# Gate and value weights split without scaling in place, and the low halves of block zero's M made on TensorE

## The chip, the core and the metric

One core of a Trainium2 chip. The metric is device microseconds of one execution, and the time of a kernel is the median of its runs. Engines are named as in the profile: PE is TensorE (PEld its weight loads), DVE is VectorE, ACT is ScalarE, POOL is GpSimd, SP is the queue that issues most DMAs.

## What is computed

Three stages, each over the output of the one before.

```python
scores = scale * x @ state^T;  a  = softmax(scores);   xread = a @ state     # B=8, H=8, S=512, D=64
scores2 = scale * state @ x^T; a2 = softmax(scores2);  sread = a2 @ x        # Ns=32
x = concat([xread, sread], axis=2) -> 4352 rows of 512
x = (sigmoid(x @ w_gate) * (x @ w_val)) @ w_out                              # 512 -> 1536 -> 512
e = argmax(x @ w_gate2);  y = softmax(x @ w_gate2)[e] * relu(x @ w1[e]) @ w2[e]   # 8 experts, 512 -> 1024 -> 512
```

The three weights of the middle stage arrive as 64-bit floats, read here as pairs of 32-bit words.

## The kernel before

Every product keeps near fp32 accuracy by splitting both operands into a high and a low float16 half and summing three products (high x high, high x low, low x high) in PSUM. To split, an operand is scaled by a power of two from its largest magnitude. `pair` (L310) does it: ScalarE writes the high half, and the low half is the difference. With `s` and not `inplace` the difference is one VectorE operation that scales and subtracts (L319). With `inplace` ScalarE first scales the fp32 operand where it lies (L313), casts it (L315), and POOL subtracts (L316).

**Weights.** Gate and value weights come in six pairs of 256 columns (`fp` = 0 to 5). `load_wgv` (L519) loads a pair raw, into regions of `wgv` and `wout` that are not yet in use. `conv_wgv` (L532) is a generator of two steps. The first joins the words with three VectorE operations per half (L499, L502, L505, each 128x1024) into a buffer of the tag `big` or `out`, and squares it on ScalarE for the largest magnitude (L540). The second spreads the maximum through a TensorE matmul (`spread`, L199), makes the scale on VectorE (L154 to L158) and calls `pair` in place (L546). The output weights go the same way in twelve pieces of 128x512 (`conv_wout`, L551), with one scale over all of them, so the scaled halves (L589, L590) come only after all twelve are joined.

**Tokens.** The rows of `xread` are not formed. For each batch b the state is multiplied into the weights instead: `state_weights` (L468) makes M, for a pair fp, by 24 small matmuls of 64x32 weights (L483) into two PSUM banks; ScalarE evacuates each bank as the high half (L490), VectorE as the low half (L491). `gate_val` (L659), for one of twelve column groups fc, multiplies M with the transposed attention aT in twelve matmuls of 512 columns (L665 to L667), six for gate and six for value. ScalarE applies the sigmoid (L671), VectorE multiplies (L673), ScalarE casts the high half (L678) and POOL subtracts the low half (L679). Four output products of 36 matmuls each follow (`mlp_out`, L717). PSUM for these is one pool of four banks (`mm_p`, L171); a gate product takes two, an M two.

**Order.** TensorE's order is the program's. `token_block` (L1095) writes it: calls of `gate_val` with a hook `mid` in the middle and at the end of each, in which numbered slots start steps of the next block's attention and of background work. On the other engines a planner orders the instructions from modelled times; each queue runs in that order.

**Block zero** (b = 0) is special: its M is made inside the loop over fc, just before its use, at each even fc (L1166 to L1172), and the weights of pair fp + 2 are converted in the same loop: the first step at fc = 2 fp (L1174, L1175), the second at fc = 2 fp + 1 (L1179). Pairs 0 and 1 are converted ahead of it (L1193 to L1201). From slot 13 on the hooks also run `conv_wout`; what is left of it is issued before the output products (L1182). For b > 0 the six Ms of the next block are made in slots GV + 2m, among the output products (L1131).

**Row metadata.** In the expert stage each tile of 128 rows has a small tile `meta` (eight of them, L874) that a DMA on SP fills (L883), and that a VectorE operation (L921) and the indirect DMA that stores the rows (L924) read.

Of the kernel before, what the change touches and what calls it, by code (L numbers as in the profile page):

```python
# [10 lines left out]
F16 = mybir.dt.float16  # L11
# [8 lines left out]
P = 128  # L20
# [6 lines left out]
def attention_moe_router_kernel(  # L27
# [49 lines left out]

    ACT_SH = 23

    SC_SH = 22  # L80

    PR_SH = 14

# [19 lines left out]
    identf = const.tile([P, P], F32, name="identf", tag="identf")  # L103
    ident = const.tile([P, P], F16, name="ident", tag="ident")
    identb = const.tile([P, P], BF16, name="identb", tag="identb")
    tri = const.tile([P, P], F16, name="tri", tag="tri")
    ones = const.tile([P, 1], F16, name="ones", tag="ones")
    iota_e = const.tile([P, NE], F32, name="iota_e", tag="iota_e")
# [22 lines left out]
        kw = {} if bufs is None else {"bufs": bufs}  # L131
        return (pool or tiny).tile(shape, dt, name=name, tag=name, **kw)

    def pow2_scale(m, k, nm, lim=40, inv=True, bufs=None, out=None):

        n = m.shape[1]
        a = tl([P, n], I32, nm + "a")
        s = tl([P, n], I32, nm + "s", bufs) if out is None else out.bitcast(I32)
        nc.vector.tensor_scalar(a, m.bitcast(I32), EXPO, EXPO, ALU.bitwise_and, ALU.bitwise_xor)
        nc.vector.tensor_scalar(  # L140
            s, a, float((128 + lim) * ONE), float((k - 1) * ONE), ALU.min, ALU.add
        )
        if not inv:
            return s.bitcast(F32), None
        c = tl([P, n], I32, nm + "c", bufs)
        nc.vector.tensor_scalar(c, s, -1.0, float(254 * ONE), ALU.mult, ALU.add)
        return s.bitcast(F32), c.bitcast(F32)

    def pow2_scale_sq(q, c, nm):
# [86 lines left out]
    def state_max(b):  # L236

        g = states[b]
        m = tl([P, 1], name="sgm")
        nc.vector.tensor_reduce(  # L240
            m, g["st"].rearrange("p r d -> p (r d)"), axis=AX.X, op=ALU.max,
            apply_absolute_value=True,
        )
        yield
        r = all_max(spread(m), "sgr")
        g["s"], g["i"] = pow2_scale(r, 14, "sg", bufs=3)

        bf = att.tile([64, H // 2, 2, D], F32, name="bf", tag="a")
        bd = att.tile([64, 2, H // 2, 2, D], F16, name="bd", tag="sT")
        bsh = [64, H // 2, 2, D]  # L250
        nc.gpsimd.tensor_tensor(
            bf, g["st"][0:64].unsqueeze(2).to_broadcast(bsh),
            hmask[0:64].unsqueeze(3).to_broadcast(bsh), op=ALU.mult,
        )
        bw = bd.rearrange("p l r i d -> p l (r i d)")
        pair(bf.rearrange("p r i d -> p (r i d)"), bw[:, 0], bw[:, 1], g["s"][0:64])
        g["bd"] = bd
        yield
# [28 lines left out]
    def unit_max(n):  # L287
# [13 lines left out]

        for nm in ("c1", "c2", "c3", "n1"):
            u[nm] = tl([P, 1], name="s" + nm, bufs=3)
        nc.vector.tensor_scalar(u["c1"], i, g["i"], SCALE, ALU.mult, ALU.mult)
        nc.vector.tensor_scalar(u["n1"], u["c1"], -1.0, None, ALU.mult)
        nc.vector.tensor_scalar(u["c2"], u["c1"], 2.0 ** SC_SH, None, ALU.mult)
        nc.vector.tensor_scalar(u["c3"], i, 2.0 ** -PR_SH, None, ALU.mult)
# [160 lines left out]
    def state_weights(b, fp):  # L468

        Mt[b, fp] = m_p.tile([P, NU, 2, 2, FP], F16, name="M", tag="M")
        pm = [mm_ps([P, 2, FP]) for c in range(NU)]
        bdT = states[b]["bdT"]
        for m, l in ((0, 0), (0, 1), (1, 0)):
            for r in range(NP):
                for h in range(2):
                    for c in range(NU):  # L480
                        k = slice(64 * h, 64 * h + 64)
                        o = NS * (h ^ c)
                        nc.tensor.matmul(  # L483
                            pm[c][64 * r + o:64 * r + o + NS],
                            bdT[k, m, NP * c + r, o:o + NS], wgv[k, fp, l, :, NP * c + r, :],
                            start=(m + l == 0), stop=(m == 1),
                        )
        t = Mt[b, fp]
        for c in range(NU):
            last["A"] = nc.scalar.activation(t[:, c, 0], pm[c], AF.Copy, scale=2.0 ** -M_SH)  # L490
            last["D"] = nc.vector.scalar_tensor_tensor(  # L491
                t[:, c, 1], pm[c], 2.0 ** -M_SH, t[:, c, 0], op0=ALU.mult, op1=ALU.subtract
            )


    def convert64(dst, raw):
# [35 lines left out]
    def conv_wgv(fp, raws):  # L532
# [10 lines left out]
        both = inv_w.rearrange("p k (a i) -> p k a i", i=2)[:, :, fp]  # L543
        s = pow2_scale_sq(r, both, "ws")
        for k in range(2):
            pair(v[k], h[k][0], h[k][1], s[:, k:k + 1], inplace=True)  # L546
        yield

    wo_sq = const.tile([P, NFC], F32, name="wo_sq", tag="wo_sq")
# [314 lines left out]
            nc.sync.dma_start(out=dst, in_=src, **kw)  # L864

    rows = {}
    xgT = {}

    def place_rows(s, late=False):
        if late:  # L870
            xgT[s] = m_p.tile([P, 2, NDC, P], F16, name="M", tag="M")
        else:
            xgT[s] = big([P, 2, NDC, P], F16)
        rows[s] = const.tile([P, 16], I32, name=f"meta{s % 8}", tag=f"meta{s % 8}")  # L874

    def fetch_rows(s, r0):
        if s not in xgT:
# [61 lines left out]
    make_identity(nc, identf)  # L939
    nc.vector.tensor_copy(ident, identf)  # L940
    nc.vector.tensor_copy(identb, identf)
    hm_i = tl([P, H // 2, 2], I32, "hm_i")

    nc.gpsimd.iota(
# [150 lines left out]
    def token_block(b):  # L1095
# [8 lines left out]
        if b + 1 < B:  # L1104
# [23 lines left out]
                at(EARLY, lambda: first_step(NU * (b + 2)))  # L1128
                at(EARLY + 2, lambda: unit_load(NU * (b + 2) + 1))
            for m in range(NFP):  # L1130
                at(GV + 2 * m, lambda m=m: state_weights(b + 1, m))  # L1131
        if b + 1 == B:
            rs = state_rows()
            at(6, lambda: next(rs, None))
# [30 lines left out]
        for fc in range(NFC):  # L1165
            if b == 0 and fc % 2 == 0:  # L1166
                fp = fc // 2
                state_weights(0, fp)
                nc.vector.tensor_scalar(
                    sg[:, fc:fc + 2], inv_w[:, 0, fc:fc + 2], isig, 2.0 ** (M_SH - PR_SH),  # L1170
                    ALU.mult, ALU.mult,
# [6 lines left out]
            elif b == 0 and fc // 2 + 2 < NFP:  # L1178
                drain(deque([cvs.pop(fc // 2 + 2)]))  # L1179
            gate_val(fc, S, sg, V_SH, token_chunks(b, fc), acts, mid)  # L1180
        if b == 0:
            drain(bg)  # L1182
        rt_new(b, isig)
# [284 lines left out]
```

## Time and profile before

| what | value |
|---|---|
| median of 3 runs | 1202.6 us (1199.43 to 1203.38) |
| the profiled execution | 1203.0 us |
| its span, first to last instruction | 1201.3 us |
| mean granted clock of TensorE | 0.952 of full |
| TensorE matmul busy in the span | 1077.0 us, 90% |
| VectorE busy | 858.8 us, 71% |
| ScalarE busy | 560.1 us, 47% |
| POOL busy | 310.1 us, 26% |

The profile comes from one execution. Rows give start and duration in microseconds from the span's start, with the line of the kernel; names are of tiles, `out<-in`. In square brackets stands how long the engine had been idle before an instruction and what ended that. A group's row gives its count, its busy time, the mean of one in ns and the idle time before its members. Matmuls overlap in their pipeline, so the listed duration of one is longer than its step to the next. The granted clock is a share of 2.4 GHz.

### The profile page before, as it was taken

To read this page: it belongs to the slowest core of one execution; us is meant where nothing else is said; L and a number is where in the kernel's file an instruction comes from. 1 tells how busy PE (TensorE), PEld (TensorE's weight loads), DVE (VectorE), ACT (ScalarE), POOL (GpSimd) and SP (SyncE) were. 2 spreads that over 40 slices of the span, in tenths; PEclk is the share of its full clock that TensorE was granted. 3 is DMA by queue.
4 is the path that set the end of the run, shared out by engine and by line. 5 is a ranking of instruction groups with operands and counts; after the bars stand their busy time and mean duration, and the time that the engine had idled before them with its cause. 6 is when DMAs were issued, how large, how long until landed. Compare 5 with 4: busy or idle time off the path is not lost. (4 is left out here: it accounts for less than half of the span.)

```text
span 1201.3 us, 22322 instructions
## 1 busy us (share of the span) xinstructions
PE 1077.0 (90%) x8303; PEld 589.6 (49%) x8303; DVE 858.8 (71%) x2079; ACT 560.1 (47%) x967; POOL 310.1 (26%) x305
## 2 busy tenths in 40 slices
PE   2265659889899999999999999999999999999997
PEld 1221224434344444344444444867666667776674
DVE  6878996688787887887877765447656666565564
ACT  3566563774776857767678483311111111111111
POOL 1244310350532524415235071301100000000000
PEclk9576779999999999999999999999999999999999
DMA  7422566545756667557465652473312495979348
GB/s 254 162 71 88 158 114 120 124 162 140 218 168 176 224 142 216 167 159 237 121 207 158 159 195 95 139 232 120 88 42 50 109 357 127 312 248 366 81 82 292
DMA packets 187745, 200.65 MB, mean 167 GB/s; under 512 B 130159, under 2 KB 154735, under 8 KB 184304
## 3 DMA queue, kind: packets, MB, share of 16 engines
q1 hardware_dynamic: 172736, 147.51, 45.0%
q0 software_dynamic: 14896, 51.67, 11.3%
q8 instruction: 67, 1.10, 0.4%
q14 instruction: 46, 0.38, 0.1%
HBM read 217.40 MB, written 54.88 MB: 227 GB/s over the span
## 5 line engine op out<-in xcount | busy, mean ns | idle before, releaser
L910 ACT CAST acth<-v 128x256 f16<-128x256 f32 x148 | 59.9, 404 | 331.2 <-DVE v L909 308.3
L679 POOL TENSOR_TENSOR actl<-g,acth 128x512 f16<-128x512 f32 (+1 forms) x108 | 138.7, 1286 | 161.8 <-ACT acth L678 161.3
L665 PE MATMUL mm<-aT,M 128*128 128x512 f16 x384 | 152.8, 398 | 26.1 <-ACT M L490 19.9
L722 PE MATMUL mm<-wout,acth 128*128 128x512 f16 x408 | 156.2, 383 | 9.1 <-DVE wout L590 8.8
L667 PE MATMUL mm<-aT,M 128*128 128x512 f16 x384 | 152.2, 396 | 11.5 <-DVE M L491 11.5
L723 PE MATMUL mm<-wout,acth 128*128 128x512 f16 x408 | 156.0, 382 | 0.0
L724 PE MATMUL mm<-wout,actl 128*128 128x512 f16 x408 | 155.8, 382 | 0.0
L666 PE MATMUL mm<-aT,M 128*128 128x512 f16 x384 | 152.7, 398 | 0.0
L895 PEld LDWEIGHTS <-wgv 128*128 128x128 f16 x1184 | 115.6, 98 | 20.0 <-DMA wgv<-w_d 2.8
L924 POOL DMA_INDIRECT out_dram<-g,meta x37 | 35.9, 972 | 344.5 <-DVE g L921 286.7
L895 PE MATMUL mm<-big,wgv 128*128 128x256 f16 x704 | 118.5, 273 | 1.5 <-DMA wgv<-w_d 1.5
L898 PEld LDWEIGHTS <-wgv 128*128 128x128 f16 x1184 | 115.8, 98 | 3.8
L898 PE MATMUL mm<-big,wgv 128*128 128x128 f16 x704 | 117.4, 219 | 0.0
L908 DVE TENSOR_REDUCE v<-mm 128x256 f32<-128x512 f32 x148 | 101.4, 685 | 19.8 <-PE mm L898 18.8
L911 DVE TENSOR_TENSOR actl<-v,acth 128x256 f16<-128x256 f32 x148 | 62.8, 424 | 68.6 <-ACT acth L910 68.6
L319 DVE SCALAR_TENSOR_TENSOR out<-big,inv,out 128x1024 f16<-128x1024 f32 x64 | 83.5, 1305 | 36.7 <-ACT out L318 36.7
L673 DVE SCALAR_TENSOR_TENSOR g<-mm,g 128x512 f32<-128x512 f32 (+1 forms) x108 | 70.9, 657 | 53.3 <-PE mm L667 27.3
L318 ACT ACTIVATE out<-big,inv 128x1024 f16<-128x1024 f32 x64 | 73.2, 1144 | 52.6 <-DVE inv L140 45.5
L671 ACT ACTIVATE g<-mm,sgf 128x512 f32<-128x512 f32 (+1 forms) x108 | 71.2, 660 | 43.5 <-POOL actl L679 26.4
L650 POOL DMA_DIRECT2D w_d<-out x63 | 35.5, 563 | 189.3 <-DVE out L319 138.1
L678 ACT CAST acth<-g 128x512 f16<-128x512 f32 (+1 forms) x108 | 63.3, 588 | 40.8 <-DVE g L673 40.6
L895 PE MATMUL mm<-out,wgv 128*128 128x256 f16 x480 | 80.8, 273 | 0.0
(320 smaller groups left out, 2152.3 us busy)
## 6 DMA issues: line engine op xcount, KB each, us to landing
wgv<-w_d SPq DMA_DIRECT2D x56, 2048.0 KB
wout<-w_d SPq DMA_DIRECT2D x18, 2048.0 KB
big<-in_moe_w_dram SPq DMA_DIRECT2D x64, 512.0 KB
w_d<-out POOLq DMA_DIRECT2D x64, 512.0 KB, 4.9
xb<-in_x_dram SPq DMA_DIRECT2D x60, 128.0 KB
wgv<-in_moe_w_gate_dram SPq DMA_DIRECT2D x3, 1024.0 KB
wgv<-in_moe_w_val_dram SPq DMA_DIRECT2D x3, 1024.0 KB
wout<-in_moe_w_gate_dram SPq DMA_DIRECT2D x3, 1024.0 KB
```

The lines of the kernel that those rows point to most:

```text
L318: nc.scalar.activation(h16, v, AF.Copy, scale=s)
L319: nc.vector.scalar_tensor_tensor(l16, v, s, h16, op0=ALU.mult, op1=ALU.subtract)
L665: nc.tensor.matmul(ps[k], w[0], v[0], start=(i == 0), stop=False)
L666: nc.tensor.matmul(ps[k], w[0], v[1], start=False, stop=False)
L667: nc.tensor.matmul(ps[k], w[1], v[0], start=False, stop=(i == len(parts) - 1))
L679: last["P"] = nc.gpsimd.tensor_tensor(lo, g, h, op=ALU.subtract)
L722: nc.tensor.matmul(po, hj, wout[:, fc, 1], start=(fc == 0), stop=False)
L723: nc.tensor.matmul(po, hj, wout[:, fc, 0], start=False, stop=False)
L724: nc.tensor.matmul(po, lj, wout[:, fc, 1], start=False, stop=(fc == NFC - 1))
L895: nc.tensor.matmul(ph[:, i], w1s[:, pr, c, 0, f], t[:, :, c], start=(c == 0), stop=False)
L898: nc.tensor.matmul(ph[:, i, 1], w1s[:, pr, c, 1, f], t[:, 0, c], start=False, stop=(c == NDC - 1),)
L908: nc.vector.tensor_reduce(v, ph.rearrange("p i l q -> p i q l"), axis=AX.X, op=ALU.add)
```

## The change

The change has four parts.

1. `conv_wgv` calls `pair` without `inplace`: ScalarE scales and writes the high half in one pass, and VectorE makes the low half (L319's operation) from the unscaled operand. L313, L315 and POOL's L316 are no longer issued for the gate and value weights.
2. `state_weights` becomes a generator of two steps. The first makes the product and lets ScalarE write the highs; for b > 0 VectorE writes the lows there as before, and callers run both steps at once. For b = 0 the second step takes two more banks, multiplies the highs by a negative scaled identity (`minus`) into them, adds the same product again and lets ScalarE write the lows.
3. In block zero M of pair 0 is made whole before the first `gate_val`; the first step for pair fp + 1 comes after `gate_val(2 fp)`, the second after `gate_val(2 fp + 1)`.
4. So that the negative identity fits float16, the state is scaled by 2^6 less (`ST_SH`), and constants are adapted. The eight `meta` tiles become slices of one tile of tag `xT`.

```diff
-    SC_SH = 22
+    ST_SH = 6
+
+    SC_SH = 22 - ST_SH
...
+    minus = const.tile([P, P], F16, name="minus", tag="minus")
...
-        g["s"], g["i"] = pow2_scale(r, 14, "sg", bufs=3)
+        g["s"], g["i"] = pow2_scale(r, 14 - ST_SH, "sg", bufs=3, sh=ST_SH)
...
+        bdT = states[b]["bdT"]
+        t = Mt[b, fp]
+        down = 2.0 ** (ST_SH - M_SH)
+
+        def product(pm, first):
+            for m, l in ((0, 0), (0, 1), (1, 0)):
+                for r in range(NP):
+                    for h in range(2):
+                        for c in range(NU):
+                            k = slice(64 * h, 64 * h + 64)
+                            o = NS * (h ^ c)
+                            nc.tensor.matmul(
+                                pm[c][64 * r + o:64 * r + o + NS],
+                                bdT[k, m, NP * c + r, o:o + NS], wgv[k, fp, l, :, NP * c + r, :],
+                                start=(first and m + l == 0), stop=(m == 1),
+                            )
+
         pm = [mm_ps([P, 2, FP]) for c in range(NU)]
...
+        product(pm, True)
         for c in range(NU):
-            last["A"] = nc.scalar.activation(t[:, c, 0], pm[c], AF.Copy, scale=2.0 ** -M_SH)
-            last["D"] = nc.vector.scalar_tensor_tensor(
-                t[:, c, 1], pm[c], 2.0 ** -M_SH, t[:, c, 0], op0=ALU.mult, op1=ALU.subtract
-            )
+            last["A"] = nc.scalar.activation(t[:, c, 0], pm[c], AF.Copy, scale=down)
+            if b > 0:
+                last["D"] = nc.vector.scalar_tensor_tensor(
+                    t[:, c, 1], pm[c], down, t[:, c, 0], op0=ALU.mult, op1=ALU.subtract
+                )
+        yield
+        if b == 0:
+            pm = [mm_ps([P, 2, FP]) for c in range(NU)]
+            for c in range(NU):
+                nc.tensor.matmul(pm[c], minus, t[:, c, 0], start=True, stop=False)
+            product(pm, False)
+            for c in range(NU):
+                nc.scalar.activation(t[:, c, 1], pm[c], AF.Copy, scale=down)
...
-            pair(v[k], h[k][0], h[k][1], s[:, k:k + 1], inplace=True)
+            pair(v[k], h[k][0], h[k][1], s[:, k:k + 1])
...
-        rows[s] = const.tile([P, 16], I32, name=f"meta{s % 8}", tag=f"meta{s % 8}")
+        if "all" not in meta:
+            meta["all"] = att.tile([P, 8, 16], I32, name="meta", tag="xT")
+        rows[s] = meta["all"][:, s % 8]
...
+    nc.vector.tensor_scalar(minus, identf, -(2.0 ** (M_SH - ST_SH)), None, ALU.mult)
...
-                at(GV + 2 * m, lambda m=m: state_weights(b + 1, m))
+                at(GV + 2 * m, lambda m=m: drain(deque([state_weights(b + 1, m)])))
...
-                state_weights(0, fp)
+                if fp == 0:
+                    ws = state_weights(0, 0)
+                    drain(deque([ws]))
...
             gate_val(fc, S, sg, V_SH, token_chunks(b, fc), acts, mid)
+            if b == 0 and fc + 2 < NFC:
+                if fc % 2 == 0:
+                    ws = state_weights(0, fc // 2 + 1)
+                next(ws, None)
```

## Rows read from the trace of the kernel before

**Rows 1.** The page, span in forty slices: busy share of each in tenths.

```profile
PE   2265659889899999999999999999999999999997
```

**Rows 2.** Windows: stretch, length, busy by engine, granted clock, DMA share, GB/s.

```profile
60.00:105.00 45.00, 26.73 (x153) 9.06 (x151) 35.96 (x52) 30.27 (x45) 20.82 (x11) 0.66 0.18 59
105.00:165.00 60.00, 31.59 (x201) 10.92 (x199) 51.78 (x112) 37.73 (x68) 19.62 (x12) 0.75 0.43 127
...
180.00:240.00 60.00, 56.65 (x498) 26.75 (x495) 39.71 (x143) 31.71 (x53) 13.20 (x11) 0.97 0.56 121
```

**Rows 3.** Waits of PE, 60 to 165: us in total, times, longest.

```profile
PE mm L665 <- ACT M L490: 19.9, 6, 6.8
PE mm L667 <- DVE M L491: 11.5, 7, 3.0
PE mm L483 <- ACT g L671: 3.7, 1, 3.7
```

**Rows 4.** Timeline of PE: start, us, instruction, idle before it and releaser.

```profile
57.45 2.72 PE L451 MATMUL at<-a2T,xn 128*128 128x64 f16 x48 [4.92 <-ACT a2T L442]
...
60.42 1.48 PE L483 MATMUL mm<-wgv,bdT 64*32 64x512 f16 x24
64.97 0.61 PE L665 MATMUL mm<-aT,M 128*128 128x512 f16 x1 [3.07 <-ACT M L490]
...
165.14 0.61 PE L722 MATMUL mm<-wout,acth 128*128 128x512 f16 x1 [6.96 <-DVE wout L590]
```

**Rows 5.** Timeline of ACT, the same columns.

```profile
55.35 1.06 ACT L540 ACTIVATE wgv<-big 128x1024 f16<-128x1024 f32 x1 [7.21 <-DVE big L505]
...
89.72 1.15 ACT L313 ACTIVATE big<-big,wss 128x1024 f32<-128x1024 f32 x1 [3.34 <-DVE wss L157]
```

**Rows 6.** Timeline of all engines, 45 to 55.

```profile
48.09 4.71 DVE L499 TENSOR_SCALAR big<-wgv 128x1024 int32<-128x1024 int32 x1 [0.72 <-POOL wgv L316]
...
50.12 2.12 POOL L316 TENSOR_TENSOR wgv<-big,wgv 128x1024 f16<-128x1024 f32 x1
```

**Rows 7.** Instructions of lines L499, L505, L319: shortest, median, longest in ns, first and last start.

```profile
L499 DVE TENSOR_SCALAR wout<-out x6: 407/414/1608, 103.8 to 129.5; 128x512 int32<-128x512 int32 x6
...
L499 DVE TENSOR_SCALAR big<-wout x2: 680/1344/2008, 89.7 to 96.9; 128x1024 int32<-128x1024 int32 x2
L499 DVE TENSOR_SCALAR out<-wout x1: 2598/2598/2598, 68.1 to 68.1; 128x1024 int32<-128x1024 int32 x1
...
L499 DVE TENSOR_SCALAR big<-wgv x1: 2214/2214/2214, 85.2 to 85.2; 128x1024 int32<-128x1024 int32 x1
...
L505 DVE SCALAR_TENSOR_TENSOR wout<-out,wout x6: 671/680/2058, 106.0 to 136.0; 128x512 int32<-128x512 int32 x6
...
L505 DVE SCALAR_TENSOR_TENSOR big<-wout,big x2: 1226/2129/3032, 93.4 to 101.1; 128x1024 int32<-128x1024 int32 x2
...
L319 DVE SCALAR_TENSOR_TENSOR bd<-bf,sgs,bd x2: 744/1610/2475, 8.3 to 132.5; 64x512 f16<-64x512 f32 x2
```

**Rows 8.** Groups of POOL by form, 60 to 165: busy, mean ns, idle before.

```profile
L679 POOL TENSOR_TENSOR actl<-g,acth 128x512 f16<-128x512 f32 x12 | 17.4, 1451 | 36.4 <-ACT acth L678 36.4
L316 POOL TENSOR_TENSOR wgv<-big,wgv 128x1024 f16<-128x1024 f32 x6 | 13.8, 2321 | 11.5 <-ACT wgv L315 11.5
L316 POOL TENSOR_TENSOR wgv<-out,wgv 128x1024 f16<-128x1024 f32 x4 | 9.3, 2344 | 17.0 <-ACT wgv L315 16.9
```

**Rows 9.** Groups of ACT by form, 60 to 165, the same columns.

```profile
L490 ACT ACTIVATE M<-mm 128x512 f16<-128x512 f32 x14 | 7.8, 587 | 0.0
```

**Rows 10.** Groups of DVE by form, 60 to 165, the same columns.

```profile
L491 DVE SCALAR_TENSOR_TENSOR M<-mm,M 128x512 f16<-128x512 f32 x14 | 9.3, 680 | 1.1 <-ACT M L490 1.1
L673 DVE SCALAR_TENSOR_TENSOR g<-mm,g 128x512 f32<-128x512 f32 x12 | 8.2, 684 | 7.1 <-PE at L199 3.4 <-PE mm L667 2.9 <-ACT g L671 0.8
L505 DVE SCALAR_TENSOR_TENSOR wout<-out,wout 128x512 int32<-128x512 int32 x6 | 6.8, 1129 | 0.0
```

**Rows 11.** Waits of the SP queue, 60 to 180.

```profile
SPq L557 <- POOL wgv L316: 33.3, 4, 23.9
```

More of the change, by code (lines that the diff above doesn't have):

```diff
@@ L132, in tl, with pow2_scale @@
         return (pool or tiny).tile(shape, dt, name=name, tag=name, **kw)
-    def pow2_scale(m, k, nm, lim=40, inv=True, bufs=None, out=None):
+    def pow2_scale(m, k, nm, lim=40, inv=True, bufs=None, out=None, sh=0):
         n = m.shape[1]
@@ L145, in pow2_scale @@
         c = tl([P, n], I32, nm + "c", bufs)
-        nc.vector.tensor_scalar(c, s, -1.0, float(254 * ONE), ALU.mult, ALU.add)
+        nc.vector.tensor_scalar(c, s, -1.0, float((254 - sh) * ONE), ALU.mult, ALU.add)
         return s.bitcast(F32), c.bitcast(F32)
@@ L303, in unit_max @@
             u[nm] = tl([P, 1], name="s" + nm, bufs=3)
-        nc.vector.tensor_scalar(u["c1"], i, g["i"], SCALE, ALU.mult, ALU.mult)
+        nc.vector.tensor_scalar(u["c1"], i, g["i"], SCALE * 2.0 ** ST_SH, ALU.mult, ALU.mult)
         nc.vector.tensor_scalar(u["n1"], u["c1"], -1.0, None, ALU.mult)
@@ L474, in state_weights @@
         Mt[b, fp] = m_p.tile([P, NU, 2, 2, FP], F16, name="M", tag="M")
-        pm = [mm_ps([P, 2, FP]) for c in range(NU)]
[L476 to L486, printed above, removed]
-                        )
@@ L488, in state_weights @@
-        t = Mt[b, fp]
-        for c in range(NU):
-            last["A"] = nc.scalar.activation(t[:, c, 0], pm[c], AF.Copy, scale=2.0 ** -M_SH)
-            last["D"] = nc.vector.scalar_tensor_tensor(
-                t[:, c, 1], pm[c], 2.0 ** -M_SH, t[:, c, 0], op0=ALU.mult, op1=ALU.subtract
-            )
+        bdT = states[b]["bdT"]
[13 more added lines that the diff above has]
+                            )
@@ L866, in attention_moe_router_kernel @@
     rows = {}
+    meta = {}
     xgT = {}
```

## The prediction

> **What bounds the kernel now.** I read the page's forty slices first [rows 1]: TensorE is at 0.8 to 0.9 of every slice from the seventh on, and at 0.2 to 0.6 in the six before. The windows say the same in microseconds [rows 2]: from 180 to 240 us TensorE is busy 56.65 of 60 at a granted clock of 0.97, between 60 and 165 us (block zero's gate and value products) only 58.3 of 105 (26.73 + 31.59) at 0.66 and 0.75 (time at the 1.2 GHz level pulls those down). So time can be won before 165 us, and once TensorE has its block zero inputs, the rest of the program follows rigidly behind it; the edited lines run for blocks one to seven as they did.
>
> The waits of TensorE in that stretch come next [rows 3]: 19.9 us for M's high halves from ScalarE and 11.5 us for M's low halves from VectorE, 31.4 us together. That is what the eye sees. But VectorE is busy 35.96 + 51.78 = 87.7 of the 105 us [rows 2], and TensorE's wait for ScalarE is often a wait for VectorE at one remove: ScalarE's queue stands still 3.34 us at 89.72 for a scale from VectorE [rows 5], in the same stretch in which TensorE waits up to 6.8 us for one high [rows 3]. So I sum over VectorE and use TensorE's waits only as a ceiling.
>
> VectorE's time is not all work. At 48.09 us a tensor_scalar took 4.71 us [rows 6]; the same operation on the same 1024 columns takes 0.68 at its shortest [rows 7]. It ended at 52.8, just after POOL's subtraction of the gate and value highs that began at 50.12 and took 2.12 [rows 6]; ten more of those follow, at 2.3 us each [rows 8]. The longest of each shape in rows 7 are such cases; their excess over the shortest of the same shape is what comes back if that work leaves POOL.
>
> **The change, part by part.**
>
> *A, up to the first product of M (60.42 us) [rows 4].* Pair zero's two subtractions leave POOL, so the stretch of 4.71 - 0.68 = 4.0 us [rows 6, 7] goes; two lows come to VectorE, at the duration of a 1024-column operation with two tensors in SBUF, 1.23 each (the shortest of L505's pair) [rows 7], 2.5 together. They fall into VectorE's pauses while TensorE transposes (the 4.71 us operation heads the chain that holds ScalarE for 7.21 us at 55.35, then the a2T copy, then TensorE for 4.92 us at 57.45) [rows 4, 5]. The attention's own subtractions stay on POOL and may still hold VectorE. I take 4.0 us earlier; bounds 2 (both lows in the way) and 6 (ScalarE, relieved of two passes, also hands over earlier).
>
> *B, the first M takes a second pass.* Nothing covers it: TensorE has no other work there. Added between the product and the first gate matmul: the second high (0.59) [rows 9], two subtracting matmuls (at the 0.61 of the matmul at 64.97, close behind each other, so about 0.6 to 1.0 for the two) and 24 small ones (1.48 for 24) [rows 4], then the low's 0.59 partly under the two matmuls that need only highs. VectorE's low, which stood in the same place, is gone. About +2.5 us; bounds 1.5 and 4. The other five Ms pay their product under waits that exist.
>
> *C, from there to 165.14 us, by VectorE's queue.* Off: 12 lows of M at 9.3/14 = 0.66 [rows 10] (two of the 14 belong to block one), 8.0 us. On: 10 weight lows (pairs one to five) at 1.21 to 1.23, 12.1 us. Off: the stretches [rows 7, 10], 1.9 + 1.5 + 1.3 (L499 with 1024 columns), 1.2 (one L499 with 512), 1.8 (L505 with 1024), 2.7 (L505 with 512: six took 6.8 in place of six times 0.68) and 1.7 (bd), 12.1 us. VectorE's work thus falls by 8.0 us. Against it, the new lows read two tensors in SBUF like L505 and can be held by what stays on POOL, the act subtractions, 17.4 us of the 105 [rows 8]: 10 lows, a chance of one in six, half of 1.45 each: 1.2 us. VectorE is also idle 17.3 of the 105 us, 6.3 of them because the evacuation of a gate product waited for TensorE [rows 10]; with TensorE no longer behind M, most of that fills, and I take 5 us off, with bounds 0 and 12 (nearly all but the loads). C = -8.0 + 1.2 - 5.0 = -11.8.
>
> What hides the rest: ScalarE gives up one pass of 1.15 us for each of ten halves [rows 5] and takes 12 lows of 0.59 [rows 9], 4.4 us less in all, so it is no new bound. M's second product, 24 small matmuls and two of 512 columns per pair, stands before the next gate product and issues no DMA: 2.1 to 2.5 us of TensorE by the rows of B, half that at the full clock, covered while VectorE is the slower; with that cover gone it would cost five times that, 6 to 12 us, which is one reason why TensorE's 31.4 us are a ceiling. The output weights' loads on the SP queue stood 33.3 us behind POOL's subtractions [rows 11]; the buffers are now freed by VectorE's lows, so they come earlier and don't hold. The state's smaller scale changes immediates only, the constant for the subtraction is one small operation in the setup, and moving the row metadata into one shared tile touches a stage in which TensorE is the bound; I cost these at nothing, and if a metadata load then waited for an older reader, the row of that load would show it.
>
> What is late next: a pair's weight lows are queued two gate products ahead of M's product that reads them, where before it was three, so TensorE will wait for the weight lows and for a gate product's banks in place of M. That is in C, since both end with VectorE.
>
> *Sum:* -4.0 + 2.5 - 11.8 = -13.3 us. The profiled execution took 1203.0 us (span 1201.3 and 1.7 around it), 0.4 above the median of 1202.6; 1203.0 - 13.3 is 1189.7, and I say 1189.5.
>
> **The rivals.**
>
> *M was the bound after all.* If all of TensorE's 31.4 us for M go and VectorE keeps up, the time is 1203.0 - 4.0 + 2.5 - 31.4 + 6 for second products = 1176. For it: those waits are the largest of the stretch. Against it: VectorE would have to do 87.7 - 8 = 79.7 us of work in 104.7 + 2.5 - 31.4 + 6 = 81.8, all but without idling.
>
> *The banks.* Each gate product now has a product of M between it and the next, so by the order of the four banks it writes the pair that the product before it filled, and waits until ScalarE and VectorE have emptied it. Such a wait is there once before, 3.7 us for ScalarE's g [rows 3]. Eleven products could meet it; at three of them with 3.7 us, 11.1 us, it takes C's gain and leaves 1203.0 - 13.3 + 11.1 = 1201, at one of them 1193. It decides if g's evacuation comes later than half a product plus M's product after the last matmul. The Trainium skill (Perfetto Trace Analysis, Optimizing Tensor Performance) asks that independent matmul groups rotate through different banks so that the evacuation of one overlaps the next, which speaks against this order.
>
> *Slower: VectorE takes the lows and gets no stretch back.* If POOL's remaining subtractions (17.4 us, and the attention's) hold the same operations as long as those that leave, A has +2.5 in place of -4.0 and C is 12.1 - 8.0 = +4.1, with B +2.5: +9.1, 1212. It decides where the L499 and L505 of rows 7 keep their long cases. Against it: of POOL's 40.5 us in the stretch, 23.1 leave [rows 8]. The Trainium skill (Perfetto Trace Analysis, Identifying the Most-Contended Engine) takes VectorE's occupancy as a fair measure of its load; read so, with 84% here, more work on it costs its full price, and this is the result. The 4.71 us for a 0.68 us operation [rows 6] differ from that.
>
> *The change does nothing that counts.* If the output weights' chain (loads, conversion, one scale over all twelve) sets 165.14 whatever M does, TensorE only waits longer there than the 6.96 us it does now [rows 4], and the time is about 1202.
>
> **How the numbers follow.** Forecast, 1183 to 1197: 0.58. M the bound (1176): 0.10. Banks: 0.13, of which 0.07 is still faster (1193 to 1199) and 0.06 not. Slower (1212): 0.12. Nothing that counts: 0.07. A measurement of this kernel tells about 0.3% from no change, 3.6 us: 1199.0 to 1206.2. So faster 0.75 (0.58 + 0.10 + 0.07), same 0.13, slower 0.12. The unknowns' bounds give -6 + 1.5 - 8 - 12 = -24.5 and -2 + 4 - 6.8 = -4.8, that is 1178 to 1198; the range goes to 1200 to take in part of the banks, and leaves out 1176, 1201 and 1212.
>
> **What would show it.** Right: no L316 of wgv on POOL, L499 and L505 at their shortest, M's first product near 56.5 us, the first output matmul near 152, VectorE busy near 80 of the shorter stretch, and after 180 us the same rows shifted. Wrong: the stretches remain (slower); gate matmuls that wait for g (banks); the first output matmul early but waiting for wout (nothing that counts); or a gain before 165 us that is lost between 180 and 300.

## Result and profile after

| | before | after |
|---|---|---|
| median, runs of one comparison | 1201.0 us (1197.4 to 1203.4) | 1184.2 us (1180.5 to 1188.4) |
| ratio of the times, 95% interval | | 0.9876 (0.9833 to 0.9920) |
| a second comparison | 1199.5 us | 1184.8 us, 0.9873 (0.9840 to 0.9905) |
| profiled execution, its span | 1203.0 us, 1201.3 us | 1188.4 us, 1186.4 us |
| first product of M starts | 60.42 us | 52.88 us |
| first gate matmul starts | 64.97 us | 58.71 us |
| first output matmul starts | 165.14 us | 149.91 us |
| from there to the end of the span | 1036.2 us | 1036.5 us |

The change makes the kernel about 1.2% faster, and all of the gain of the profiled execution lies ahead of the first output matmul: 15.2 us there, and 0.3 us the other way behind it. (The code behind that matmul is nearly the same in all versions of this case, and there the remainder runs from 1027.7 to 1036.6 us; so close an agreement is in part chance.) Lines of the changed kernel have moved: M's product is L489, M's highs L498, the subtracting matmuls L507, M's lows L510, the gate matmuls L682 to L684, the output matmuls L739 to L741, the joins L516, L519 and L522, the square for the maximum L557, `pair` L319 (POOL), L321 (ScalarE) and L322 (VectorE). The windows of the stretch from the first product of M to the first output matmul, and of 60 us of block zero's output products, which answer to [rows 2] (length, busy of PE, PEld, DVE, ACT and POOL, granted clock, DMA share, GB/s):

```profile
52.88:149.91 97.03, 61.97 (x503) 21.41 (x503) 83.79 (x166) 65.13 (x114) 20.53 (x14) 0.79 0.38 112
180.00:240.00 60.00, 52.68 (x357) 23.49 (x354) 35.82 (x125) 34.87 (x56) 17.88 (x16) 0.94 0.37 106
```

In the first row TensorE is busier than before, VectorE and ScalarE a little less, and POOL half as busy as its 40.4 us were. The second row isn't at the same place of the program as the row of before; moved by the 15.2 us, before has 53.51 us of TensorE at 0.97 in 195.23 to 255.23.

TensorE's waits in that stretch (total, times, longest), which answer to [rows 3]:

```profile
PE mm L684 <- ACT M L510: 13.8, 5, 4.2
PE at L202 <- DVE wom L595: 5.8, 1, 5.8
PE mm L682 <- ACT g L688: 3.9, 1, 3.9
PE mm L507 <- ACT M L498: 3.1, 1, 3.1
PE mm L507 <- DVE g L690: 2.2, 1, 2.2
```

The waits for M's halves went from 31.4 us to 17.6 (13.8 + 3.1 and a last 0.7 for a high). The other two large waits stand at the end of the stretch, for the output weights: the matmul that spreads their largest magnitude waits 5.8 us, and the first output matmul, outside the window by its start, 5.5 us for their scaled halves. TensorE's last rows before the output products:

```profile
137.56 0.84 PE L489 MATMUL mm<-wgv,bdT 64*32 64x512 f16 x24
144.17 0.29 PE L202 MATMUL at<-identb,wom 128*128 128x128 bf16 x1 [5.77 <-DVE wom L595]
149.91 0.61 PE L739 MATMUL mm<-wout,acth 128*128 128x512 f16 x1 [5.45 <-DVE wout L607]
```

TensorE is through with block zero's gate products and block one's first M at 138.4, and then stands still for 11.2 of 11.5 us until VectorE has the output weights ready (9.9 us before the change, 2.92 and 6.96 [rows 4]). So a wait for M that goes is not by itself a gain: it can come back here. The timeline of TensorE, then that of VectorE and of ScalarE, which answer to [rows 4 to 6]:

```profile
47.67 1.91 PE L444 MATMUL at<-ident,xT 128*128 128x128 f16 x16
49.87 2.18 PE L454 MATMUL at<-a2T,xn 128*128 128x64 f16 x48 [0.28 <-DVE aT L433]
...
52.88 0.84 PE L489 MATMUL mm<-wgv,bdT 64*32 64x512 f16 x24
56.85 0.86 PE L507 MATMUL mm<-M,minus 128*128 128x512 f16 x2 [3.13 <-ACT M L498]
57.65 1.13 PE L489 MATMUL mm<-wgv,bdT 64*32 64x512 f16 x24
58.71 0.61 PE L682 MATMUL mm<-aT,M 128*128 128x512 f16 x1
```

```profile
46.12 1.64 DVE L516 TENSOR_SCALAR big<-wgv 128x1024 int32<-128x1024 int32 x1
```

```profile
48.77 1.93 ACT L445 COPY a2T<-at 128x1024 f16<-128x1024 f16 x2 [1.21 <-PE at L444]
...
53.85 1.06 ACT L557 ACTIVATE wgv<-big 128x1024 f16<-128x1024 f32 x1 [1.13 <-DVE big L522]
```

The join that took 4.71 us takes 1.64, and ScalarE's a2T copies now run ahead of the square L557 and start as the transposes deliver. The instructions of two join lines and of the new lows (shortest, median, longest in ns, first and last start), which answer to [rows 7]:

```profile
L516 DVE TENSOR_SCALAR wout<-out x6: 408/424/1386, 91.3 to 115.8; 128x512 int32<-128x512 int32 x6
L516 DVE TENSOR_SCALAR wout<-big x6: 408/416/427, 102.4 to 129.7; 128x512 int32<-128x512 int32 x6
...
L522 DVE SCALAR_TENSOR_TENSOR wout<-out,wout x6: 671/684/1645, 93.6 to 120.9; 128x512 int32<-128x512 int32 x6
...
L322 DVE SCALAR_TENSOR_TENSOR wgv<-big,wss,wgv x8: 1268/1280/2049, 42.2 to 111.9; 128x1024 f16<-128x1024 f32 x8
L322 DVE SCALAR_TENSOR_TENSOR wgv<-out,wss,wgv x4: 1276/1281/1285, 58.4 to 95.6; 128x1024 f16<-128x1024 f32 x4
```

The medians are now near the shortest, and single long cases are left. What is left on POOL in the stretch, its largest group (count, busy, mean ns, idle before), which answers to [rows 8]:

```profile
L696 POOL TENSOR_TENSOR actl<-g,acth 128x512 f16<-128x512 f32 x12 | 18.3, 1529 | 74.0 <-ACT acth L695 74.0
```

**VectorE's account.** For every profiled kernel I split VectorE's time from the span's start to the first output matmul into three. *Held* is what each instruction took beyond the shortest of the same operation, tiles and shape in any of the profiles; *work* is the rest of its busy time; *idle* is what is left. Of the held time, 25.3 of 27.5 us before and 11.3 of 13.7 after lie on instructions that overlap one of POOL's. The forecast's column adds the terms of A, B and C; under idle stand the 5.0 of C, the 2.5 of A's two lows, which were to fall into pauses, and the 2.5 of B, for which VectorE waits.

| us | before | after | difference | forecast |
|---|---|---|---|---|
| first output matmul | 165.1 | 149.9 | -15.2 | -13.3 |
| held | 27.5 | 13.7 | -13.8 | -14.9 (4.0 + 12.1 - 1.2) |
| work | 106.5 | 114.7 | +8.1 | +6.6 (2.5 + 12.1 - 8.0) |
| idle | 31.1 | 21.5 | -9.5 | -5.0 (-5.0 - 2.5 + 2.5) |

### The profile page after: what moved, and what is told of

The parts are those of the page before. It is cut to its first block, busy times and chain, and to the rows that moved or that the text cites. A ratio compares the mean times of both kernels' runs of the same rounds, so it can differ in the third digit from the quotient of the medians.

```text
span 1186.4 us, 22619 instructions
## 1 busy us (share of the span) xinstructions
PE 1083.8 (91%) x8459; PEld 592.4 (50%) x8459; DVE 852.7 (72%) x2080; ACT 554.4 (47%) x967; POOL 284.8 (24%) x293
## 3 DMA queue, kind: packets, MB, share of 16 engines
q0 software_dynamic: 14896, 51.67, 11.5%
## 5 line engine op out<-in xcount | busy, mean ns | idle before, releaser
L684 PE MATMUL mm<-aT,M 128*128 128x512 f16 x384 | 152.5, 397 | 13.8 <-ACT M L510 13.8
L682 PE MATMUL mm<-aT,M 128*128 128x512 f16 x384 | 152.2, 396 | 14.0 <-ACT g L688 13.3
L739 PE MATMUL mm<-wout,acth 128*128 128x512 f16 x408 | 155.6, 381 | 9.5 <-DVE wout L607 8.5
L741 PE MATMUL mm<-wout,actl 128*128 128x512 f16 x408 | 155.3, 381 | 0.0
L322 DVE SCALAR_TENSOR_TENSOR out<-big,inv,out 128x1024 f16<-128x1024 f32 x64 | 82.9, 1295 | 36.3 <-ACT out L321 36.3
L321 ACT ACTIVATE out<-big,inv 128x1024 f16<-128x1024 f32 x64 | 73.2, 1144 | 52.6 <-DVE inv L143 45.5
L688 ACT ACTIVATE g<-mm,sgf 128x512 f32<-128x512 f32 (+1 forms) x108 | 71.4, 661 | 41.2 <-POOL actl L696 30.8
L695 ACT CAST acth<-g 128x512 f16<-128x512 f32 (+1 forms) x108 | 63.3, 588 | 41.2 <-DVE g L690 41.0
```

The costliest lines, as they stand in the source:

```text
L321: nc.scalar.activation(h16, v, AF.Copy, scale=s)
L322: nc.vector.scalar_tensor_tensor(l16, v, s, h16, op0=ALU.mult, op1=ALU.subtract)
L682: nc.tensor.matmul(ps[k], w[0], v[0], start=(i == 0), stop=False)
L684: nc.tensor.matmul(ps[k], w[1], v[0], start=False, stop=(i == len(parts) - 1))
L739: nc.tensor.matmul(po, hj, wout[:, fc, 1], start=(fc == 0), stop=False)
L741: nc.tensor.matmul(po, lj, wout[:, fc, 1], start=False, stop=(fc == NFC - 1))
```

## The experiments

Two theories stood against each other at first. By V, VectorE's queue sets the stretch up to the first output matmul: every microsecond of its work and of what POOL holds of it counts, wherever it lies. By M, the order on TensorE around M sets it: when each M is asked for and when its halves are ready. Later ones are told with their runs. The table has all runs; the ratio is to the kernel before in the same comparison, the other columns are VectorE's account.

| kernel | ratio (95%) | median us | first output matmul | held | work | idle |
|---|---|---|---|---|---|---|
| before | 1 | | 165.1 | 27.5 | 106.5 | 31.1 |
| after, again | 0.9873 (0.9840 to 0.9905) | 1184.8 | 150.4 | 16.4 | 113.8 | 20.3 |
| e1: split alone | 0.9916 (0.9892 to 0.9941) | 1190.5 | 154.0 | 15.0 | 120.9 | 18.1 |
| e2: lead and M's lows by TensorE, no split | 1.0090 (1.0057 to 1.0123) | 1211.2 | 172.5 | 29.6 | 101.7 | 41.2 |
| e12: lead alone | 1.0089 (1.0060 to 1.0118) | 1209.7 | 175.8 | 29.8 | 107.5 | 38.5 |
| e3: no lead | 0.9958 (0.9935 to 0.9980) | 1194.2 | 161.5 | 13.5 | 114.5 | 33.5 |
| e4: M's lows on VectorE | 0.9865 (0.9843 to 0.9887) | 1183.2 | 150.3 | 13.7 | 121.7 | 14.9 |
| e9: half of the Ms each way | 0.9880 (0.9846 to 0.9915) | 1184.7 | 151.5 | 10.9 | 118.8 | 21.7 |
| e7: M's lows half a product earlier | 0.9868 (0.9834 to 0.9902) | 1183.7 | 149.5 | 17.7 | 113.9 | 17.9 |
| e10: e4, 12 more lows on VectorE | 0.9944 (0.9920 to 0.9967) | 1194.1 | 158.3 | 17.7 | 127.2 | 13.5 |
| e11: e4, 12 more passes on ScalarE | 0.9892 (0.9850 to 0.9934) | 1188.6 | 149.4 | 12.7 | 120.1 | 16.6 |
| e6: two passes on ScalarE | 0.9976 (0.9951 to 1.0001) | 1196.6 | 158.8 | 11.4 | 114.7 | 32.6 |
| e5: POOL kept busy | 1.0044 (1.0019 to 1.0069) | 1203.6 | 169.9 | 30.2 | 114.0 | 25.7 |

"Split" is the first part of the change (gate and value weights without scaling in place), "lead" the third (M made one product ahead). All but e1 keep the fourth part (the smaller scale and the shared metadata tile).

**The change again.** The same kernel, to see how far two comparisons and two profiles agree.

> The changed kernel as it is, beside the runs of this call on the same chip: 0.9876 of before again, so that the version with M's lows on VectorE (0.9865) can be told from it to half a per cent. If TensorE's lows are worth nothing the two lie within 4 us.

The ratios agree to 0.0003; the two profiles differ by 0.5 us in the first output matmul and by 2.7 us in held.

**e1, the split alone**, on the kernel before:

```diff
-            pair(v[k], h[k][0], h[k][1], s[:, k:k + 1], inplace=True)
+            pair(v[k], h[k][0], h[k][1], s[:, k:k + 1])
```

> The kernel before, with the weights' split alone changed (one ScalarE pass, lows on VectorE). Theory V (VectorE's queue sets block zero, with the time that POOL holds it): the way to M's first product shortens as in the changed kernel, 7.5 us; after that VectorE gets 10 lows (13 us) and is given back some 9 us of held time, M's lows stay on it, so +4: about 3.5 us faster than before, 1197.5. Theory M (TensorE's waits for M set it): the weights matter only up to the first product, 7.5 us faster, 1193.5, and the 31 us of waits for M are all still there.

It gives 0.0084 of the change's 0.0127, two thirds, and was faster than either theory had it. Held falls by 12.5, work rises by 14.3 (twelve lows at 1.27 are 15.2, less what shifts over the boundary), and idle falls by 12.9. So the held time that leaves does not quite pay for the lows; the gain comes because VectorE idles less. TensorE's waits (as above):

```profile
PE mm L665 <- ACT M L490: 14.6, 6, 4.8
PE mm L667 <- DVE M L491: 9.4, 4, 3.3
PE mm L483 <- ACT g L671: 6.9, 1, 6.9
```

**e12, the lead alone**: e4 (below) with `inplace=True` put back. **e2, lead and TensorE lows**, the changed kernel with

```diff
-            pair(v[k], h[k][0], h[k][1], s[:, k:k + 1])
+            pair(v[k], h[k][0], h[k][1], s[:, k:k + 1], inplace=True)
```

> The changed kernel, with the weights scaled in place and their lows on POOL as before; M's lows on TensorE and the lead stay. V: no gain up to the first product, +1.3 for the first M's second pass, VectorE's work 8 us less and a few us less idle time, POOL's subtractions still hold it: about 10 us faster than before, 1191. M: the waits for M go and are partly replaced by the 14 us for the lows that the changed kernel shows, so 31 - 14 - 1.3 = 16 us faster, 1185; if the weights' lows from POOL are late for the earlier product, TensorE waits for those by name and the gain is lost, 1200.

> The lead alone: weights scaled in place with POOL's lows as in the kernel before, M's lows on VectorE, M one gate product ahead. With the weights' split the lead was worth 6 us. If it is worth that by itself: 1195. If the lead needs the weights early, since M's product now asks for them a gate product sooner and POOL's chain is late, it is worth nothing or less: 1201 to 1206, with TensorE waiting for the weights by name.

Both are slower than before by 0.9%, and slower than any of their forecasts. Held stays (29.6 and 29.8), idle grows by 10.1 and 7.5 us. TensorE's waits in e12:

```profile
PE mm L489 <- ACT wgv L318: 14.3, 4, 5.8
PE mm L489 <- POOL wgv L319: 13.7, 5, 3.7
```

and VectorE's in e2 (who waits, for what; total, times, longest):

```profile
DVE big L516 <- POOL wgv L319: 8.5, 2, 6.0
...
DVE out L516 <- POOL wgv L319: 3.5, 1, 3.5
```

The lead makes TensorE ask for a pair's weights one product earlier, and 28.0 us of e12's waits are for those weights, high and low, at the end of the chain of two ScalarE passes and POOL. VectorE for its part waits for the buffers that POOL frees last. The lead needs the split; with it the lead is worth 0.0051 (e4 against e1, which also lacks the fourth part).

**e3, no lead**: the changed kernel with both steps of M at once at each even fc:

```diff
-                if fp == 0:
-                    ws = state_weights(0, 0)
-                    drain(deque([ws]))
+                drain(deque([state_weights(0, fp)]))
...
-            if b == 0 and fc + 2 < NFC:
-                if fc % 2 == 0:
-                    ws = state_weights(0, fc // 2 + 1)
-                next(ws, None)
```

> The changed kernel without the lead: each M of block zero is made whole, both passes, right before the gate product that uses it. V: VectorE's work is that of the changed kernel, only its idle time grows back to that of before, 4 us: 1188. M: five more Ms stand on the path with 4.5 to 5.8 us each, as the first one does: 22 to 29 us slower than the changed kernel, 1206 to 1213.

Between the two: 1194.2 us. Against e1, which has no lead either but its lows on VectorE, TensorE's lows cost 0.0042. The largest wait:

```profile
PE mm L507 <- ACT M L498: 24.3, 6, 5.4
```

Product, high, subtraction and product again stand in a row six times, with nothing between them. The wait alone is not the loss, for e1 waits as long for M (14.6 + 9.4). What e3 has more is TensorE's second pass, uncovered: TensorE is busy 63.56 of 107.01 us from the first product of M to the first output matmul, in e1 55.90 of 100.85, so 7.7 us more in a stretch 6.2 us longer. VectorE's idle time is 15.4 us above e1's.

**e4, M's lows on VectorE as before**, split and lead kept:

```diff
-            if b > 0:
-                last["D"] = nc.vector.scalar_tensor_tensor(
+            last["D"] = nc.vector.scalar_tensor_tensor(
...
-        if b == 0:
-            pm = [mm_ps([P, 2, FP]) for c in range(NU)]
...
```

> The changed kernel with M's lows of block zero back on VectorE and no second product on TensorE; the lead stays (product, highs and lows one gate product ahead), and so does the weights' split. V: VectorE's work is 8 us more, the first M is 1.3 us shorter: 6 to 7 us slower than the changed kernel, 1191. M: the lows are ready one gate product earlier than now, so the 13.8 us that TensorE waits for them go too: 1184 or less, down to 1172.

The time is at the upper end of where M had it, and this is the run that fells V's way of counting. VectorE has 7.0 us more work than in the changed kernel and 6.6 us less idle; the time is the same within the intervals, which leave room for some 4 us between the two, not for 7. Its window, of the same columns as above, and its waits on TensorE and on VectorE:

```profile
53.50:150.27 96.77, 53.10 (x347) 19.49 (x346) 90.65 (x178) 59.50 (x104) 19.72 (x14) 0.76 0.36 109
```

```profile
PE at L202 <- DVE wom L587: 9.2, 1, 9.2
PE mm L489 <- ACT wgv L321: 9.1, 4, 4.5
PE mm L489 <- DVE wgv L322: 7.2, 4, 4.0
PE mm L674 <- DVE M L499: 6.0, 2, 5.7
```

```profile
DVE wgv L322 <- ACT wgv L321: 1.0, 3, 0.4
```

VectorE is busy 90.65 of 96.77 us here: its queue has hardly a gap (6.1 us in all). In the changed kernel it has gaps, of which the largest are

```profile
DVE wgv L322 <- ACT wgv L321: 4.3, 4, 1.7
DVE wout L516 <- DMA big<-in_moe_w_out_dram: 3.9, 1, 3.9
```

These two are 6.7 us more than in e4 (1.0 and 0.5). They say where part of the idle time stands; that TensorE's second product caused each of them isn't shown.

**e9, half of the Ms each way, and e7, the lows earlier.** In e9 pairs 0 to 2 have their lows on VectorE and 3 to 5 on TensorE (`if b > 0 or fp < 3` for VectorE's low, `if b == 0 and fp > 2` for the second pass). In e7 the second step of M runs at the first hook of the odd product, half a product earlier (`half` counts the hooks):

```diff
+            def mid0():
+                if b == 0 and fc % 2 and half[0] == 2 * fc:
+                    next(ws, None)
+                mid()
+
-            gate_val(fc, S, sg, V_SH, token_chunks(b, fc), acts, mid)
+            gate_val(fc, S, sg, V_SH, token_chunks(b, fc), acts, mid0)
...
-                next(ws, None)
+                    next(ws)
```

> The changed kernel with M's lows of pairs 0 to 2 on VectorE (one gate product ahead) and of pairs 3 to 5 on TensorE. Both whole versions took the same time, one with VectorE busy 94% of the stretch, the other with TensorE waiting for lows. If VectorE's load is what the first lacks and the uncovered first pass what the second lacks, this one beats both: 1178 to 1181. If the planner's order decides, no better than either: 1184.

> The changed kernel with the second pass of each M ahead by half a gate product more: it stands in the middle of the odd gate product instead of behind it. TensorE's waits for ScalarE's lows (13.8 us in five) fall by about 1.3 each. If those waits set the stretch: 6 us faster than the changed kernel, 1178. If VectorE and the output weights set it: within 2 us of it, 1183.

Neither differs from the changed kernel. e7 tests TensorE's largest wait: L684 for M's low falls from 13.8 us to

```profile
PE mm L684 <- ACT M L510: 2.9, 3, 2.0
```

and the first output matmul starts at 149.5 us, 0.4 earlier; waits for the highs (5.2), a gate product's bank (3.8) and the weights (3.6 + 3.4) stand in its place. Of what is gained on the way, 1.2 us are left at block one's M (136.34 in place of 137.56), and there TensorE waits longer for the output weights, 12.1 us (6.62 + 5.45) in place of 11.2.

**e10 and e11, which queue sets e4's stretch.** Both add to e4, for block zero (`if b == 0`), one more operation on each of the twelve banks of M, written to a scrap tile that nobody reads (its slice is left out here):

```diff
+                nc.vector.scalar_tensor_tensor(junk8[...], pm[c], down, t[:, c, 0], op0=ALU.mult, op1=ALU.subtract, saturate=False)
```

in e10, and in e11

```diff
+                nc.scalar.activation(junk8[...], pm[c], AF.Copy, scale=down, saturate=False)
```

> The version with M's lows of block zero on VectorE, one gate product ahead (1183), with each such low made a second time into a scrap tile that nobody reads: 12 more operations of 0.66 us on VectorE, 8 us. VectorE is idle only 6.9 of 96.8 us there. If VectorE's queue sets the stretch, nearly all of it shows: 1189 to 1191. If the way of each pair's weights through ScalarE and TensorE sets it: 1183 to 1185.

> The same version, with one more ScalarE pass of 0.59 us per bank of M into a scrap tile: 12 more operations, 7 us, which is what M's lows on TensorE cost ScalarE in the changed kernel, without the second product. If ScalarE's queue is where the changed kernel loses the 7 us that VectorE was relieved of, this one is 5 to 7 us slower than the version it is made from, 1189. If the loss is TensorE's second product and its place in the order, nothing shows: 1183.

Twelve times 0.68 us are 8.2 us; e10's first output matmul starts 8.1 us later than e4's. ScalarE's twelve passes raise its busy time there by 6.4 us (86.1 to 92.5), and the first output matmul starts 0.9 us earlier. e11's median is 5 us above e4's, but its interval holds e4's ratio, so what it costs in the end stays open; in the stretch it costs nothing. So in e4 VectorE's queue is the bound, at its full price. In the changed kernel, which has 7 us less work on it and is no faster, it can't be the only one.

**e6, the split with ScalarE's two passes kept**, the changed kernel with the subtraction on VectorE but scale and cast apart:

```diff
-            pair(v[k], h[k][0], h[k][1], s[:, k:k + 1])
+            nc.scalar.activation(v[k], v[k], AF.Copy, scale=s[:, k:k + 1])
+            nc.scalar.copy(h[k][0], v[k])
+            nc.vector.tensor_tensor(h[k][1], v[k], h[k][0], op=ALU.subtract)
```

> The changed kernel with ScalarE's second pass back (scale in place, then cast) and the subtraction on VectorE: ScalarE's load and order as before, POOL unloaded. If POOL was the point: about 1185 (ScalarE is busy 65 of 97 us in the stretch and has room for 11 more). If ScalarE's pass was the point, each pair's weights come 2.2 us later and its queue holds M and g as long: 11 us more, 1195. Against the run with both passes and POOL (1211) it says what POOL alone does.

About 12 us slower than the changed kernel: nearly the whole gain is gone, though held (11.4) is lower than there and work (114.7) the same. ScalarE is busy 10.6 us more (92.2 to 102.7), VectorE idles 11.1 us more. Its two largest waits in the stretch are for ScalarE; of the first the changed kernel has nothing, of the second 4.3 us:

```profile
DVE g L692 <- ACT g L690: 6.2, 2, 4.2
DVE wgv L565 <- ACT wgv L564: 5.5, 3, 4.6
```

The pass that ScalarE loses is thus a condition of the gain in this kernel, although ScalarE is busy for only two thirds of the stretch. Against e2, which has both passes and the subtraction on POOL, e6 is faster by 0.0114, some 14 us: so much is the subtraction's move from POOL to VectorE worth here, and the pass about as much again, each to about 5 us by the intervals. Whether its time counts, or that high and low come one pass later, e6 doesn't tell; with M's lows on VectorE it wasn't tried.

**What stands after these.** Neither theory does as it was put. M's is right that the lows leaving VectorE earn nothing, wrong that TensorE's waits for M are what counts (e7). V's is right where VectorE's queue is full (e4, e10), wrong for the changed kernel, where 7 us off VectorE's queue earned nothing (e4, e9) and 10.6 us more on ScalarE cost 12 (e6). That VectorE, ScalarE and TensorE wait for each other in turn there is read from the waits; no run shows it by itself. What carries the gain is the shorter way of the weights (e1), and the last run asks whether POOL's hold on VectorE is part of it.

**e5, POOL kept busy.** The changed kernel, and after each weight half a subtraction on POOL that reads the high half twice and writes a scrap tile:

```diff
             pair(v[k], h[k][0], h[k][1], s[:, k:k + 1])
+            nc.gpsimd.tensor_tensor(junk8, h[k][0], h[k][0], op=ALU.subtract, saturate=False)
```

> The changed kernel, plus one subtraction of 128x1024 on POOL behind each high of the gate and value weights, into a scrap tile that nobody waits for: POOL is loaded as before, but the weights don't depend on it. If the time that POOL holds VectorE is what the split's change gave back, some 9 us return in block zero: 1192, with L516 and L522 at their long durations again. If only the length of the chain through ScalarE and POOL counted, nothing returns: 1184.

It is slower than before: 20 us above the changed kernel by the ratios, 20.0 us in the first output matmul, twice what was expected. Work is the same to 0.7 us, idle is up 4.2, held is up 16.5 us, of which 7.4 lie on the new lows and 7.7 on the joins L516 and L519. POOL's added group (columns as above), and the timeline at the first of them:

```profile
L564 POOL TENSOR_TENSOR junk<-wgv 128x1024 fp8e5<-128x1024 f16 x10 | 26.1, 2612 | 13.7 <-ACT wgv L321 9.3 <-issue 4.1
```

```profile
42.58 2.07 POOL L564 TENSOR_TENSOR junk<-wgv 128x1024 fp8e5<-128x1024 f16 x1 [35.84 <-ACT wgv L321]
42.81 5.01 DVE L322 SCALAR_TENSOR_TENSOR wgv<-big,wss,wgv 128x1024 f16<-128x1024 f32 x2
```

Two lows that take 2.48 us in the changed kernel take 5.01 beside POOL, on which they depend in nothing. One by one they took 2.91 and 2.17 us: the first met the added subtraction, the second, late by that, the attention's own (44.73 us, 2.01), and each ended 1.1 us after the one that it met. So the price of POOL's subtraction is not its place in the chain alone: it stops VectorE. Ahead of M's first product POOL's own later subtractions are late as well (TensorE's wait for aq's lows goes from 1.6 to 4.8 us), so the 5.2 us there are not VectorE's alone. Behind it POOL's lateness hardly counts: ScalarE waited 0.9 us for POOL, TensorE for POOL not at all. The Trainium skill (SBUF — State Buffer, Who interferes with whom) says that a VectorE instruction with two inputs in SBUF and a GpSimd instruction that reads SBUF shut each other out, the one that issues second until the first is done; the 5.01 us agree with that.

## Why the prediction was right, and where its steps were not

The profiled execution was forecast at 1189.7 and took 1188.4; the medians of the two comparisons, 1184.2 and 1184.8, lie in the range. The forecast's sign and size hold: 13.3 us, measured 14.6 in the profiled executions and 16.9 and 14.7 in the medians. Its main reading holds as far as it goes: TensorE's waits for M were not what there was to win (e7 removes one and gains nothing), and VectorE's time held by POOL was (e5 puts it back and loses everything). But it named only half of what there was: with POOL off the weights, ScalarE's second pass alone takes back some 12 us (e6). Two terms were wrong, in opposite directions, and that the sum came out so near is in part luck.

*A, to the first product of M: forecast -4.0, bounds -2 and -6; measured -7.5.* Outside the bounds. The 4.71 us operation did shrink, to 1.64, so 3.1 of the 4.0 came back. What was missed is the order on ScalarE: a2T stood behind the square L540, which waited for that operation's chain; now it stands ahead of it, and starts at 48.77 in place of 56.41. In the kernel before, TensorE's transposes and ScalarE's copies stand in the timeline at

```profile
50.62 1.91 PE L441 MATMUL at<-ident,xT 128*128 128x128 f16 x16
```

```profile
56.41 1.90 ACT L442 COPY a2T<-at 128x1024 f16<-128x1024 f16 x2
```

Of the 7.6 us from 56.41 to 48.77, 2.95 are the transposes' (50.62 to 47.67, since POOL delivers aq's lows earlier), the other 4.7 the queue's. It isn't ScalarE's relief, to which the forecast gave its better bound: e6 keeps both passes and has its first product at 53.48, e12 and e2 keep POOL's subtractions and have it at 61.2 and 60.3.

*B, the second pass of the first M: forecast +2.5; measured +1.3* (4.55 us from product to gate matmul before, 5.83 after), a little under its bound of 1.5. The second pass itself took 1.86 (56.85 to 58.71), for the second high fell under the first subtraction and the granted clock was 0.83 there. The rest is the clock of the first product: it took 0.84 us at a granted clock of 1.00, where before it took 1.48 at 0.50. The first lows stand under the gate product's first two matmuls, as said.

*C, to the first output matmul: forecast -11.8; measured -9.0.* By terms, over the whole way: the held time is near (-13.8 against -14.9). The new lows were priced at 1.23 and take 1.27 at their shortest; the ten of the stretch are held for 0.9 us (13.6 us against ten times 1.27), where 1.2 was taken. **The step that failed is "off: 12 lows of M, 8.0 us".** The work did leave VectorE, but e4 puts it back at no cost in time: it came back as idle time of the same size. It would have been worth its price only while VectorE's queue was full, as e10 shows for e4. The other is the sentence that costs ScalarE's lost pass at nothing: e6, which keeps it, is about 12 us slower. The idle time fell by 9.5 us where 5 were taken, and most of that hangs on this pass (e6, which keeps it, idles 11.1 us longer) and on the weights being ready earlier (e1: idle down by 12.9 with the split alone). The two errors nearly cancel. Nor did what was said to be late next come so: TensorE waits for no weight lows in the changed kernel, and its largest wait is still for M (such waits stand in e4, 9.1 + 7.2).

*What was costed at nothing.* The output weights' loads wait for VectorE's lows now, as said (26.0 us of the SP queue's wait for L322 in 60 to 180); one join waits 3.9 us for such a load, where joins waited 4.5 before. The metadata tile and the smaller scale were not tried alone; behind the first output matmul the spans agree to 0.3 us, which by the spread of the other runs' remainders can't exclude a few.

**The rivals.** *M was the bound*: no; the time is the same with TensorE's wait for M's lows at 13.8 us, at 2.9 (e7) and with other waits in its place (e4). *The banks*: gate product or subtraction waited for a bank twice, 3.9 and 2.2 us, not three times or more; without the split it is the larger matter (9.2 and 7.1 us in e2). *Slower, no stretch back*: held would have had to stay; e5, where it does, is 1.0044, near the rival's mechanism if not its 1212. *Nothing that counts*: no, though its observation is right: the first output matmul still waits for its weights, 5.5 us after 6.96. That chain, for which TensorE waits last in every profile of this case (8.8 to 13.0 us together), runs through VectorE's queue and came forward with it.

No version here beats the changed kernel. e4 equals it with 309 fewer instructions (22310 against 22619), without the negative identity and the second product; of the change's four parts, the split and the lead make the gain, unless the fourth, which stands in both, has a share.

## What to carry to other kernels

Before counting an engine's busy time as its load, compare long instructions with the shortest of their kind: what the difference hides may belong to another engine, and moving that engine's work can be worth more than moving the busy engine's. A microsecond taken off the busiest queue is worth a microsecond only while that queue has no gaps; look for what would fill them before paying for the move with another engine's work. An earlier order for a consumer (the lead) must be checked against the chain that feeds it: alone it cost 0.9%, behind a shorter chain it gained 0.5%.

## What was not expected

POOL's subtraction holds VectorE even where it reads float16 alone, writes a tile that nobody reads, and VectorE depends on nothing of it: twelve of them, at 2.6 us each (ten stand in the row), raised the held time by 16.5 us and the run by 20. And ScalarE, busy 65 of 97 us, lost some 12 us with a second pass of about one microsecond per weight half (e6), while twelve of 0.6 us at another place in e4 cost nothing in the stretch (e11): its share of busy time says neither.
